# A fused spectral filter and gated FFN on one core: reordered first loads, plain-product turns, a constant filler tile, and five drains at the end

## The chip, the cores and the metric

The kernel runs on one core of one Trainium2 chip. The metric is device time in microseconds (us), lower is better. One profiled execution per kernel is quoted; its times count from the start of its span, which is about 1.8 us shorter than the device time.

Words used below: in this kernel TensorE runs the matrix products, ScalarE, VectorE and GpSimd the work on single elements, and SyncE only issues transfers and waits for semaphores. A transfer *lands* when its semaphore reports it complete. A *filler* is a matmul whose result nobody uses. The *rise* is the moment at which TensorE's granted clock goes from half to full. A *drain* is an instruction that computes nothing. The *closing checks* are SyncE's waits for semaphores at the end of the program, and its *report* is the drain with which it signals the final barrier.

## The reference

```python
x  = A_x                                   # (1, 2048, 640) bf16
xn = layernorm(x)                          # over the last axis
s  = irfft2(rfft2(xn) * (w_r + 1j*w_i))    # 2-D transform of 2048 x 640
g  = silu((gelu(xn @ w_gate) * (xn @ w_up)) @ w_down)   # F = 1536
return x + s * g
```

The sequence is split into 16 slabs of 128 rows. Gate and up projections need the input turned (rows into columns), 128 columns at a time, five pieces for a slab of 640.

## The kernel before

The kernel records every operation as a task with an estimated cost, and a planner written in Python decides the order on each engine before the program is built. So an edit of a cost, of an expected landing, or of which engine does what, can reorder work far from the edit. Parts that matter here:

```python
# fillers: matmuls on a zeroed tile that only keep TensorE busy
def blank(e):
    nc.vector.memset(place(idle, (512,)), 0.0)
...
x_in[0] = add(...)                      # slab 0 comes on ScalarE's queue
load_w(Wg, gv, g_in, 0, 2, land=4690)   # SyncE's queue, in this order
load_x(1, 2, land=5200)
load_w(Wu, uv, u_in, 0, 2, land=6790)
load_x(2, 3, land=7280)
load_x(3, 4, land=7750)
t = add(blank, "DVE", (330, 400), (0, -9), new=[idle])
t = warmed = keep_warm(6, [t])          # and 2 more after slab 0's turn
...
# turn of a raw slab: five transposes into PSUM, one copy to SBUF
for c in range(5):
    nc.tensor.transpose(out=half()[:, c*P:c*P+P], in_=X[:, n1, c*P:c*P+P], identity=ident)
...
with tc.manual_schedule():
    for t in plan.run():
        t.emit(t.on)
```

The first two tiles of gate and up work on the raw slabs and are normalised afterwards, so that TensorE need not wait for the statistics.

## Time and profile before

| quantity, kernel before | value |
|---|---|
| device time, median of the first 3 runs | 202.7 us (202.13 to 202.86) |
| span of the profiled run | 200.7 us |
| TensorE: first matmul starts, last one ends | 1.21 us, 196.76 us |
| first useful matmul, first gate matmul, first up matmul | 3.74, 5.75, 7.16 us |
| TensorE clock goes from half to full speed | 6.31 us |
| SyncE reports to the final barrier | 199.85 us |

The prediction shows the lines on which this rests.

### The profile page before, as it was taken

What the parts mean: (1) busy time and instruction counts of PE and PEld (TensorE: products, weight loads), DVE (VectorE), ACT (ScalarE), POOL (GpSimd) and SP (SyncE); (2) the same over time, 40 slices, a digit from 0 to 9 for tenths busy, and PEclk for the clock granted to TensorE, in tenths of its full rate; (3) what the DMA queues carried; (4) which work ended last, traced back from release to release, by engine and by line L of the source; (5) the groups of instructions that cost most, each with busy time, mean ns of one, the idle gap of its engine ahead of it and who ended that gap; (6) DMA issues with size and microseconds to landing.
All of it is one profiled execution on the core that took longest, in us unless ns stands there. A gap on an engine that the chain in (4) does not pass through costs nothing.

```text
span 200.7 us, 4126 instructions
## 1 busy us (share of the span) xinstructions
PE 195.5 (97%) x1527; PEld 118.2 (59%) x1527; DVE 148.6 (74%) x318; ACT 128.3 (64%) x226; POOL 32.8 (16%) x71
## 2 busy tenths in 40 slices
PE   7999999999999999999999999999999999999992
PEld 3994444667544655777755455467765555457781
DVE  3689999996524159999998999933157788787773
ACT  3899989763722767767775767233466565776451
POOL 2414333896000000000000000000004122211210
PEclk9999999999999999999999999999999999999999
DMA  6999999896639976333244110116704242332432
GB/s 180 325 316 325 339 393 225 207 257 171 207 76 349 340 179 135 92 97 122 61 118 132 68 65 1 69 64 215 309 3 141 90 134 98 102 104 92 131 103 67
DMA packets 35895, 32.63 MB, mean 163 GB/s; under 512 B 10910, under 2 KB 32930, under 8 KB 35874
## 3 DMA queue, kind: packets, MB, share of 16 engines
q1 hardware_dynamic: 34434, 29.49, 50.4%
q0 software_dynamic: 1152, 2.66, 4.9%
q10 hardware_dynamic: 288, 0.20, 0.5%
q8 instruction: 12, 0.20, 0.4%
q14 instruction: 9, 0.07, 0.1%
HBM read 22.51 MB, written 9.19 MB: 158 GB/s over the span
## 4 chain that ended last, share of the span: by engine, by line
PE 97%; DVE 0%; ACT 0%; issue 0%; DVEq 0%
PE pg L886 26%; PE pu L886 26%; PE pg L976 13%; PE pu L976 13%; PE sp L697 3%; PE sp L830 3%; PE sp L772 2%; PE sp L806 2%; PE sp L368 2%; PE sp L670 2%; PE sp L532 2%; PE sp L690 1%; PE sp L824 1%; PE sp L463 1%; PE sp L478 1%; PE sp L653 0%
## 5 line engine op out<-in xcount | busy, mean ns | idle before, releaser
L886 PE MATMUL pu<-xnT,Wu 128*128 128x512 bf16 (+1 forms) x245 | 57.6, 366 | 0.0
L886 PE MATMUL pg<-xnT,Wg 128*128 128x512 bf16 (+1 forms) x245 | 57.5, 366 | 0.0
L907 DVE TENSOR_TENSOR uT<-pu,ge 128x512 bf16<-128x512 f32 x46 | 31.8, 690 | 20.6 <-PE pu L886 17.5
L976 PEld LDWEIGHTS <-uT 128*128 128x128 bf16 x396 | 37.9, 98 | 13.5
L903 ACT ACTIVATE ge<-pg 128x512 bf16<-128x512 f32 x46 | 27.6, 599 | 24.9 <-PE pg L886 24.4
L886 PEld LDWEIGHTS <-Wg 128*128 128x128 bf16 x285 | 25.5, 99 | 22.1
L886 PEld LDWEIGHTS <-Wu 128*128 128x128 bf16 x285 | 25.0, 98 | 21.6
L976 PE MATMUL pg<-Wd,uT 128*128 128x320 bf16 (+2 forms) x204 | 30.8, 293 | 0.0
L296 ACT CAST ma<-sp 128x644 bf16<-128x644 f32 (+1 forms) x32 | 23.4, 792 | 9.7 <-PE sp L830 7.9
L976 PE MATMUL pu<-Wd,uT 128*128 128x320 bf16 (+1 forms) x192 | 29.3, 297 | 0.0
L932 POOL COPY xr<-s 1x1 bf16<-1x1 bf16 x1 | 0.2, 179 | 100.3 <-DVE s L856 100.3
L933 POOL DMA_DIRECT2D xr<-in_A_x_dram x16 | 8.8, 550 | 32.3 <-DVE res L960 30.2
L296 ACT CAST IU<-sp 128x640 bf16<-128x640 f32 x16 | 10.9, 691 | 4.2 <-PE sp L772 4.1
L296 ACT CAST Vt<-sp 128x640 bf16<-128x640 f32 x16 | 10.8, 691 | 3.7 <-PE sp L806 3.7
L296 ACT CAST mc<-sp 128x640 bf16<-128x640 f32 x16 | 10.8, 700 | 3.4 <-DMA D<-mc 2.8
L985 ACT ACTIVATE th<-pu 128x320 f32<-128x320 f32 x15 | 6.6, 438 | 9.6 <-PE pu L976 9.3
L990 DVE SCALAR_TENSOR_TENSOR G<-th,pg 128x320 bf16<-128x320 f32 x15 | 7.2, 483 | 7.1 <-ACT th L985 6.9
L985 ACT ACTIVATE th<-pg 128x320 f32<-128x320 f32 x15 | 6.7, 445 | 7.8 <-PE pg L976 7.7
L990 DVE SCALAR_TENSOR_TENSOR G<-th,pu 128x320 bf16<-128x320 f32 x15 | 7.3, 484 | 4.6 <-ACT th L985 4.4
L433 POOL TENSOR_TENSOR RSTD<-MVA,mh 128x1 f32<-128x1 f32 x12 | 9.8, 815 | 4.0 <-DVE MVA L415 3.2
L848 DVE TENSOR_TENSOR mb<-ma 128x640 bf16<-128x640 bf16 x8 | 3.9, 491 | 6.8 <-ACT ma L296 6.8
L960 DVE TENSOR_TENSOR res<-yg,xr 128x640 bf16<-128x640 bf16 (+2 forms) x18 | 8.0, 449 | 0.2
(107 smaller groups left out, 255.1 us busy)
## 6 DMA issues: line engine op xcount, KB each, us to landing
BU<-D SPq DMA_DIRECT2D x8, 640.0 KB
D<-mc SPq DMA_DIRECT2D x8, 320.0 KB
D<-IU SPq DMA_DIRECT2D x8, 320.0 KB
xr<-in_A_x_dram POOLq DMA_DIRECT2D x16, 160.0 KB, 2.6
out_dram<-res SPq DMA_DIRECT2D x15, 160.0 KB
Wg<-in_B_w_gate_dram SPq DMA_DIRECT2D x6, 320.0 KB
Wu<-in_B_w_up_dram SPq DMA_DIRECT2D x6, 320.0 KB
Wd<-in_B_w_down_dram SPq DMA_DIRECT2D x6, 320.0 KB
```

What stands on the lines that cost most here:

```text
L296: return nc.scalar.copy(out=out, in_=in_) if e == "ACT" else nc.vector.tensor_copy(out=out, in_=in_)
L433: nc.gpsimd.tensor_tensor(out=rstd, in0=var, in1=mh, op=ALU.pow)
L697: nc.tensor.matmul(into(q, ri), lhsT=sZ.tile[:, q, ri, :], rhs=FM[:, kinds[q][2] + (4 if ri and kind == 0 else 0), :], start=False, stop=T ...
L830: nc.tensor.matmul(into(q, s), lhsT=svs[s].tile[:, c, :], rhs=IM[:, q, :], start=False, stop=True, skip_group_check=True)
L886: nc.tensor.matmul(ps.tile[:, lo:hi + more], lhsT=w[:, c, t * P:(t + 1) * P], rhs=XR[:, c, lo + (lo > 0):hi + 1 if lo or more else hi] if ...
L903: nc.scalar.activation(out=ge.tile, in_=pg.tile if src is None else src, func=ACT.Gelu_apprx_tanh)
L907: nc.vector.tensor_tensor(out=u.tile, in0=pu.tile if src is None else src, in1=ge.tile, op=ALU.mult)
L933: nc.gpsimd.dma_start(out=sx.tile, in_=xv[:, n1, :])
L960: (nc.gpsimd if n1 in () else nc.vector).tensor_tensor(out=res.tile[:, lo:hi], in0=yg.tile[:, lo:hi], in1=sx.tile[:, lo:hi], op=ALU.add)
L976: nc.tensor.matmul(ps.tile[:, 0:hi - lo], lhsT=uT[grp, ks[i]].tile[:, j * P:(j + 1) * P], rhs=Wd[:, ks[i], lo:hi], start=(i == 0), stop=(i ...
L985: nc.scalar.activation(out=th.tile[:, 0:hi - lo], in_=ps.tile[:, 0:hi - lo], func=ACT.Tanh, scale=0.5)
L990: nc.vector.scalar_tensor_tensor(out=G2.tile[:, lo:hi], in0=th.tile[:, 0:hi - lo], scalar=1.0, in1=ps.tile[:, 0:hi - lo], op0=ALU.add, op1 ...
```

## The change

The intent is to give TensorE slab 1 sooner, to begin the fillers without a wait, and to shorten the end. The diff, cut:

```diff
-    def blank(e):
-        nc.vector.memset(place(idle, (512,)), 0.0)
+    ones = nc.const_aps.tensor(1.0, [P, 512], BF16)
...
-    load_w(Wg, gv, g_in, 0, 2, land=4690)
-    load_x(1, 2, land=5200)
-    load_w(Wu, uv, u_in, 0, 2, land=6790)
-    load_x(2, 3, land=7280)
-    load_x(3, 4, land=7750)
-    t = add(blank, "DVE", (330, 400), (0, -9), new=[idle])
-    t = warmed = keep_warm(6, [t])
+    load_x(1, 2, land=3990)
+    load_w(Wg, gv, g_in, 0, 2, land=4900)
+    load_x(2, 3, land=5950)
+    load_w(Wu, uv, u_in, 0, 2, land=6950)
+    load_x(3, 4, land=7450)
+    t = warmed = keep_warm(8, [], ns=395)
...
+        parts = ((0, 3), (3, 5)) if n1 < 1 else ((0, 5),)     # slab 0 in two pieces
...
+                    if n1 < 2:
+                        nc.tensor.matmul(plain(k, lo, hi)[...], lhsT=X[:, n1, c*P:c*P+P], rhs=ident, ...)
+                    else:
+                        nc.tensor.transpose(out=half(k)[...], in_=X[:, n1, c*P:c*P+P], identity=ident)
...
-    lead = ("DVE", "ACT", "DVE", "ACT")
+    lead = ('DVE', 'DVE', 'ACT', 'DVE')                       # who does the statistics
...
         for t in plan.run():
             t.emit(t.on)
+        for _ in range(5):
+            nc.sync.drain(fusable=False)
```

More of the change, by code (lines that the diff above doesn't have):

```diff
@@ L357 @@
         nc.gpsimd.memset(w[:, :, :, L:LP], 0.0)
-    idle, heat = Slot("uT"), Slot("sp")
-    def blank(e):
-        nc.vector.memset(place(idle, (512,)), 0.0)
+    heat = Slot("sp")
+    ones = nc.const_aps.tensor(1.0, [P, 512], BF16)
     def keep_warm(n, after, rank=(0, -9), ns=425):
@@ L367, in go @@
             for k in range(n):
-                nc.tensor.matmul(heat.tile[:, k % 2, :], lhsT=idle.tile[:, 0:P], rhs=idle.tile,
+                nc.tensor.matmul(heat.tile[:, k % 2, :], lhsT=ones[:, 0:P], rhs=ones,
                                  start=True, stop=True, skip_group_check=True)
-        return add(go, "PE", (n * ns, n * ns), rank, after=after, new=[] if heat.users else [heat], use=[idle] + ([heat] if heat.users else []))
+        return add(go, "PE", (n * ns, n * ns), rank, after=after, new=[] if heat.users else [heat], use=[heat] if heat.users else [])
     seq[0] += 1
-    x_in[0] = add(lambda e: None, "SP", (1, 1), (0, -5), size=1, land=3620)
-    load_w(Wg, gv, g_in, 0, 2, land=4690)
-    load_x(1, 2, land=5200)
-    load_w(Wu, uv, u_in, 0, 2, land=6790)
-    load_x(2, 3, land=7280)
-    load_x(3, 4, land=7750)
-    t = add(blank, "DVE", (330, 400), (0, -9), new=[idle])
-    t = warmed = keep_warm(6, [t])
+    x_in[0] = add(lambda e: None, "SP", (1, 1), (0, -5), size=1, land=3880)
+    load_x(1, 2, land=3990)
[4 more added lines that the diff above has]
+    t = warmed = keep_warm(8, [], ns=395)
     load_gu(2, 4)
@@ L455, in turn_raw, with half, plain, mm @@
         pt = Slot("sp")
-        def half():
-            return pt.tile[:, 0, :].bitcast(BF16)[:, 0:D]
-        def mm(e):
-            place(pt, (2, 512))
-            for c in range(5):
-                nc.tensor.transpose(out=half()[:, c * P:c * P + P], in_=X[:, n1, c * P:c * P + P], identity=ident)
-        a = add(mm, "PE", c_pe(*[140] * 5), (0, n1), after=[x_in[n1], warmed], new=[pt], use=[sX])
-        if n1 == 0:
-            keep_warm(2, [a], (0, 0, 0))
-        raw[n1] = add(lambda e: copy_on(e, XR[:, :, n1 * P + (n1 > 0):(n1 + 1) * P + (n1 > 0)], half().rearrange("p (c n) -> p c n", c=5)),
-                      {"ACT": c_act(640)} if n1 < 2 else {"ACT": c_act(640), "DVE": (415, 560)}, None, (0, n1), after=[a], use=[pt], hold={1: 1000}.get(n1, 200))
+        parts = ((0, 3), (3, 5)) if n1 < 1 else ((0, 5),)
+        t = []
+        def half(k):
+            return pt.tile[:, k, :].bitcast(BF16)[:, 0:D]
+        def plain(k, lo, hi):
+            return flat(pt.tile)[:, 512 * k:512 * k + (hi - lo) * P]
+        for k, (lo, hi) in enumerate(parts):
+            def mm(e, k=k, lo=lo, hi=hi):
+                if k == 0:
+                    place(pt, (2, 512))
+                for c in range(lo, hi):
+                    if n1 < 2:
+                        nc.tensor.matmul(plain(k, lo, hi)[:, (c - lo) * P:(c - lo) * P + P], lhsT=X[:, n1, c * P:c * P + P], rhs=ident, start=True, stop=True, skip_group_check=True)
+                    else:
+                        nc.tensor.transpose(out=half(k)[:, c * P:c * P + P], in_=X[:, n1, c * P:c * P + P], identity=ident)
+            def cp(e, k=k, lo=lo, hi=hi):
+                copy_on(e, XR[:, lo:hi, n1 * P + (n1 > 0):(n1 + 1) * P + (n1 > 0)], (plain(k, lo, hi) if n1 < 2 else half(k)[:, lo * P:hi * P]).rearrange("p (c n) -> p c n", c=hi - lo))
+            n = hi - lo
+            a = add(mm, "PE", c_pe(*[(250 if n1 < 2 else 140)] * n), (0, n1), after=[x_in[n1], warmed] + t[-1:], new=[] if k else [pt], use=[sX, pt] if k else [sX])
+            t.append(a)
+            raw[n1] = add(cp, {"ACT": c_act(128 * n)} if n1 < 2 else {"ACT": c_act(128 * n), "DVE": (83 * n, 83 * n + 145)}, None, (0, n1), after=[a], use=[pt],
+                          hold=1000 if n1 < 2 else 200)
     for n1 in range(4):
```

## The prediction

> **What bounds the kernel now.** I read the page first: the span, the busy shares, the chain that ended last.
>
> ```profile
> span 200.7 us, 4126 instructions
> ...
> PE 195.5 (97%) x1527; PEld 118.2 (59%) x1527; DVE 148.6 (74%) x318; ACT 128.3 (64%) x226; POOL 32.8 (16%) x71
> ...
> PE 97%; DVE 0%; ACT 0%; issue 0%; DVEq 0%
> ```
>
> TensorE is busy for 195.5 of 200.7 us and is 97% of the chain. It starts at 1.21 us and its last matmul ends at 196.76: 195.55 us, so it never stands still in between. I also took the start-to-start distances of all matmuls from the trace's records: from 20 to 70 us they exceed columns/2.4 + 2.5 ns by nothing, and later only concurrent small ones differ. The kernel is therefore three pieces laid end to end: a front before TensorE does useful work at full speed, about 190 us of fixed matmul work, and a tail after the last matmul. Only front, tail, or a new stall in the middle can move the time.
>
> The front, from the timeline of TensorE over the first 14 us (start, length, instruction, count), and what ScalarE does there:
>
> ```profile
> 1.21 2.74 PE L368 MATMUL sp<-uT 128*128 128x512 bf16 x6 [1.21 <-DVE uT L361]
> 3.74 0.74 PE L463 MATMUL sp<-ident,X 128*128 128x128 bf16 x5
> 4.28 1.06 PE L368 MATMUL sp<-uT 128*128 128x512 bf16 x2
> 5.27 0.69 PE L463 MATMUL sp<-ident,X 128*128 128x128 bf16 x5
> 5.75 1.00 PE L886 MATMUL pg<-XR,Wg 128*128 128x129 bf16 x10
> 6.59 0.44 PE L478 MATMUL sp<-ident,s 128*128 128x128 bf16 x5
> 6.87 0.45 PE L886 MATMUL pg<-XR,Wg 128*128 128x128 bf16 x5
> 7.16 0.73 PE L886 MATMUL pu<-XR,Wu 128*128 128x129 bf16 x10
> ```
>
> ```profile
> 4.52 0.69 ACT L296 COPY XR<-sp 128x640 bf16<-128x640 bf16 x1 [1.85 <-PE sp L463]
> 6.00 0.70 ACT L296 COPY XR<-sp 128x640 bf16<-128x640 bf16 x1 [0.78 <-PE sp L463]
> ```
>
> L368 are eight filler matmuls that only keep TensorE busy. Useful work is slab 0's five transposes (3.74), slab 1's (5.27), then ten gate matmuls (5.75). The clock is read from distances between starts: the fillers stand 0.42 us apart (2.53 / 6), half speed for 512 columns; ten gate matmuls take 0.84 us, about half of them at 107 ns and the rest at 57; from 6.59 on five take 0.28, which is 56 each. In the records the clock rises at 6.31 us. (The page's clock row shows 9 throughout and does not help here.)
>
> The waits view over 0 to 15 us names what holds the front:
>
> ```profile
> PEld L463 <- DMA X<-in_A_x_dram: 1.3, 2, 0.7
> PE sp L368 <- DVE uT L361: 1.2, 1, 1.2
> ```
>
> Slab 1 is the second of those waits. The landing records give x0 3.55 us, first gate weights 4.59, x1 5.11, first up weights 6.18, x2 6.65, x3 7.14. So x1, queued behind 320 KB of weights, comes late although the weights themselves are early. The up weights were there a microsecond before TensorE reached them.
>
> The tail, from the chain and the timeline over the last 5 us:
>
> ```profile
> 196.07 0.69 PE pg L976 x12
> ...
> 196.78 0.29 ACT G L996
> ...
> 197.09 0.29 DVE yg L953
> 197.38 0.20 DVE res L960
> ```
>
> ```profile
> 197.61 0.33 SPq L303 DMA_DIRECT2D out_dram<-res  x1
> 197.75 0.35 ACTq L965 DMA_DIRECT2D out_dram<-res  x1
> ```
>
> ```profile
> SPq L1042 <- DMA out_dram<-res: 0.8, 1, 0.8
> ```
>
> SyncE issues the last-but-one store at 197.61, then runs nine closing semaphore checks about 62 ns apart. It reaches the check of that store about 198.4 and waits 0.8 us, until 199.21. The last store's check passes at 199.37, a drain at 199.45. The next drain, which reports SyncE to the final barrier, is recorded only at 199.85, although nothing in the program stands between the two: a hole of 0.39 us where neighbours are 0.05 apart. The other engines are already waiting. 0.6 us after it begins again the DMA records show an 8 KiB transfer on the instruction queue. SyncE's earlier such transfer follows its record 80, and this hole follows record 206, about 128 instructions (8 KiB at 64 bytes) later. I read the hole as the crossing of an instruction page.
>
> **What the Trainium skill says.** "TensorE: Matmul & The Clock Gate", Part 1: start-to-start is 426.7 ns for 512 columns while cold, 215.7 once warm, and the clock rises after a busy window of about 3.4 us that runs freely, so the moment varies from run to run. The trace agrees on the distances (427 ns, 107 to 56 for 128 columns), and the rise came 5.1 us after the first matmul. The same page, Part 4: transpose-mode matmuls do not count as busy in the same way; this would be why slabs 0 and 1 become plain products. No run shows it yet, and in this trace the 3.4 us before the rise held ten transposes. "Runtime: NRT & Kernel Launch", section "Instruction fetch mechanics", has instruction memory refilled in blocks by the sequencer's own queue and the crossing "mostly hidden"; here blocks on that queue are 8 KiB and I take one crossing for unhidden. "DMA: Bandwidth & Descriptors", section on SWDGE's anatomy, puts most of the fixed cost into waiting for the last byte's receipt: here x0's last packet ended at 2.89 and it landed at 3.55.
>
> **The change part by part.**
>
> 1. Filler. The constant tile is written at 0.30, before the opening barrier. The DVE memset (0.27 us and its signal) goes. TensorE can start when the other engines do, at about 0.8 in place of 1.21. Eight fillers cold: 8 x 0.427 = 3.4, to 4.2. Their number is unchanged, but all precede slab 0; none separates the two turns.
>
> 2. Load order. x1 leads SyncE's queue and runs beside x0 on ScalarE's. It should land near x0, 3.6 to 4.0. Gate weights move from 4.59 to about 4.9; then at the steps between landings seen above (0.5 us for a slab, 1.05 for weights) x2 5.4, up weights 6.45, x3 6.95.
>
> 3. Turns and copies. A plain product streams the same 128 columns: no gain in matmul time. Slab 0 at 4.2 to 4.73, slab 1 to 5.26. Splitting slab 0 in 3 + 2 lets ScalarE copy earlier: the third product ends near 4.73, a copy of 3/5 of 640 columns is estimated at 0.46 us from the 0.69 measured, the second at 0.33. The first is done near 5.2, the second near 5.55. Gates start at 5.28 in place of 5.75, with a short wait at the fourth. F32 instead of bf16 out of PSUM: the page's own f32 copies of 640 columns are 0.69 to 0.70, so nothing.
>
> 4. What this is worth. Built, the programs have the same 3,055 TensorE rows, so matmul work is equal. In the changed order 35 useful matmuls stand ahead of the first up matmul, 30 before (slab 2's turn moved ahead). With the clock rising at 6.31 as now, gates end at 6.33, slab 2's turn 6.61, slab 1's gates 6.89, the transpose of normalised slab 0 at 7.17. TensorE reaches the up weights at 7.17 against 7.16, five matmuls ahead: 5 x 56 = 0.28 us. If the clock rises a filler earlier, gates end at 6.0 and the point comes at about 6.98: 0.28 + 0.18 = 0.46. I choose 0.4, as continuous activity begins 0.4 us sooner. The new statistics roles (slab 1 on VectorE, slab 2 on ScalarE) put four copies and slab 2's statistics on ScalarE; I expect at most a 0.1 us wait, at slab 3's turn.
>
> 5. Drains. SyncE's body grows by exactly five instructions, 196 to 201, so the page crossing moves five back: from between the last two drains to the fifth and sixth closing checks. Timing: 197.99 + five drains at about 62 ns (an estimate from the neighbouring checks) + seven checks, 0.43, + 0.39 = 199.13, still before the store's landing at 199.2. So the hole hides under the store and 0.39 - 0.05 = 0.34 us leaves the tail.
>
> Sum: 0.4 + 0.34 = 0.74, and 202.7 - 0.74 = 201.96; I say 202.0, leaving a little for new waits.
>
> **The rivals.** (a) Front only: the drains cost their own time and the hole stays, because it is not a page crossing; 202.3, or 202.6 if drains add 0.3. For: the skill calls crossings hidden. Against: the distance of 128 and the fetch. (b) The clock decides: if the activity window falls so that the rise comes late, near 7.7, all work to then costs double and front gain shrinks to about 0.2; with an early rise before's own waits at 5.27 remain and the gain grows to 0.6. The 0.73 us spread of three runs before speaks for such a lottery. (c) A new stall: the whole plan after the front was recomputed and DMA order differs for tens of us. VectorE is 74% and ScalarE 64% busy with rooms in between, so I expect none, but with TensorE full nothing can absorb one: 0.3 to 1 us back, 202.3 to 203. (d) Later gate weights bind: no, 4.9 is ahead of the copy's 5.2.
>
> **Range and chances.** Best case 0.6 + 0.34 off and a lucky median gives 201.4; front 0.2 alone gives 202.5. A 2% change is 4 us, over the whole front gap: within 2% is nearly certain.
>
> **What would show it.** First filler at 0.8 and slab 1's turn directly behind slab 0's; x1 landing before 4.1; first gate matmul near 5.3; the first up matmul near 7.0 with 35 useful ones ahead; no drain hole at the end but one among the closing checks, hidden, and about 2.75 in place of 3.09 us from the last matmul's chain end (196.76) to the report of SyncE (199.85). The prediction is wrong if TensorE stands still in the middle, or the hole stays.

## The result, and the profile after

The changed kernel takes 201.9 us (median of 4 runs, 201.79 to 201.97), before 202.57 us (4 runs, 202.13 to 202.86). The ratio is 0.9968, with a 95% interval of 0.9948 to 0.9988. Ratios are the mean time of one kernel's runs over that of the other's in the same rounds, so they are not quite the ratio of the medians. 0.65 us is clear of noise.

The page of the changed kernel:

```profile
span 200.0 us, 4106 instructions
...
PE 194.5 (97%) x1508; PEld 118.0 (59%) x1527; DVE 147.7 (74%) x319; ACT 127.5 (64%) x225; POOL 31.8 (16%) x71
...
PE 97%; issue 1%; ACT 0%; DVE 0%; DVEq 0%
```

The bound has not moved. Nineteen matmul records are missing from this trace (1508 against 1527 weight loads); each shows as a false gap of one matmul.

TensorE over the first 7 us (start, length, instruction, count):

```profile
0.77 3.57 PE L367 MATMUL sp<-const-bfloat16-1.0 128*128 128x512 bf16 x8 [0.77 <-PEq L1043]
4.16 1.13 PE L468 MATMUL sp<-ident,X 128*128 128x128 bf16 x10
5.45 0.83 PE L896 MATMUL pg<-XR,Wg 128*128 128x129 bf16 x10 [0.15 <-ACT XR L296]
6.12 0.44 PE L470 MATMUL sp<-ident,X 128*128 128x128 bf16 x5
6.39 0.45 PE L896 MATMUL pg<-XR,Wg 128*128 128x128 bf16 x5
6.72 0.45 PE L488 MATMUL sp<-ident,s 128*128 128x128 bf16 x5
```

The fillers start at 0.77 and the two turns follow each other at 4.16. Gates start at 5.45 after a wait for ScalarE's copy. The first up matmul is at 7.17, with 35 useful matmuls ahead of it (10 + 10 + 5 + 5 + 5). Two of the lines that are new in the waits view over 0 to 15 us:

```profile
PEld L896 <- DMA Wu<-in_B_w_up_dram: 0.2, 1, 0.2
PE pg L896 <- ACT XR L296: 0.2, 1, 0.2
```

The first says that the up weights now hold TensorE up. They landed at 7.12, the other landings being slab 0 4.12, slab 1 3.89, gate weights 5.10, slab 2 5.50. The clock rose at 5.03.

The end of the chain of waits in the changed kernel, and SyncE's own waits from 190 us on (total, times, longest):

```profile
195.82 0.68 PE pg L986 x12
...
196.53 0.29 ACT G L1006
...
196.84 0.29 DVE yg L963
197.13 0.20 DVE res L970
```

```profile
SPq L303 <- DVE res L970: 10.7, 5, 5.1
SPq L1054 <- PEq L1054: 0.7, 2, 0.5
```

The line that before waited 0.8 us for the store is gone: SyncE arrives at that check just as the store has landed (landing 198.94, check 198.995, one step of 64 ns behind the check ahead of it). In the records of SyncE's sequencer the hole stands between the fifth closing check (198.44) and the sixth (198.85), 0.38 us; the last two drains are 0.06 apart. From the start of the last matmul to SyncE's report it takes 2.98 us, 3.32 before.

The tail gains a little more than that. The reporting drain itself took 0.114 us in the kernel before, where it comes right behind the hole, and takes 0.007 now. From the start of the last matmul to the end of the span it is 3.74 us, 4.20 before.

So the profiled pair, whose spans differ by 0.71 us, splits into 0.25 us of front (the last matmul starts at 196.28 against 196.53) and 0.46 us of tail.

### The profile page after: what moved, and what is told of

It reads as the page before. It is cut to its first block, busy times and chain, and to the rows that moved or that the text cites. A ratio compares the mean times of both kernels' runs of the same rounds, so it can differ in the third digit from the quotient of the medians.

```text
span 200.0 us, 4106 instructions
## 1 busy us (share of the span) xinstructions
PE 194.5 (97%) x1508; PEld 118.0 (59%) x1527; DVE 147.7 (74%) x319; ACT 127.5 (64%) x225; POOL 31.8 (16%) x71
## 4 chain that ended last, share of the span: by engine, by line
PE 97%; issue 1%; ACT 0%; DVE 0%; DVEq 0%
PE pu L896 26%; PE pg L896 25%; PE pg L986 13%; PE pu L986 13%; PE sp L707 3%; PE sp L840 3%; PE sp L782 2%; PE sp L816 2%; PE sp L680 2%; PE sp L367 2%; PE sp L542 2%; PE sp L834 1%; PE sp L700 1%; PE sp L488 1%; PE sp L543 0%
## 5 line engine op out<-in xcount | busy, mean ns | idle before, releaser
L896 PE MATMUL pg<-xnT,Wg 128*128 128x512 bf16 (+1 forms) x231 | 55.7, 365 | 0.5
L986 PE MATMUL pu<-Wd,uT 128*128 128x320 bf16 (+1 forms) x192 | 29.8, 297 | 0.0
L296 ACT CAST Z<-sp 128x1024 bf16<-128x1024 f32 x8 | 7.9, 1013 | 2.5 <-PE sp L680 2.5
L431 POOL TENSOR_TENSOR RSTD<-MVA,mh 128x1 f32<-128x1 f32 x12 | 8.2, 686 | 2.8 <-DVE MVA L413 2.1
L409 DVE BATCH_NORM_STATS2 STAT<-X 128x6 f32<-128x320 bf16 x12 | 5.5, 482 | 3.7 <-DMA X<-in_A_x_dram 3.7
```

Of the source, the lines that this page charges most:

```text
L296: return nc.scalar.copy(out=out, in_=in_) if e == "ACT" else nc.vector.tensor_copy(out=out, in_=in_)
L409: nc.vector.bn_stats(out=STAT[:, n1, 6 * g:6 * g + 6], in_=x[:, 320 * g:320 * g + 320])
L431: nc.gpsimd.tensor_tensor(out=rstd, in0=var, in1=mh, op=ALU.pow)
L896: nc.tensor.matmul(ps.tile[:, lo:hi + more], lhsT=w[:, c, t * P:(t + 1) * P], rhs=XR[:, c, lo + (lo > 0):hi + 1 if lo or more else hi] if ...
L986: nc.tensor.matmul(ps.tile[:, 0:hi - lo], lhsT=uT[grp, ks[i]].tile[:, j * P:(j + 1) * P], rhs=Wd[:, ks[i], lo:hi], start=(i == 0), stop=(i ...
```

## The experiments

Twelve kernels ran in three calls, each beside fresh runs of the kernel before on the same chip. All were correct. Six runs each, eleven of before per call (medians 202.69, 202.73, 202.59).

To compare fronts I use one number: the moment by which TensorE has reached 35 useful matmuls. It is the start of the first up matmul, plus 56 ns for each useful matmul short of 35 ahead of it.

| kernel | ratio to before (95%) | clock rise | first gate | 35 useful by | last matmul starts | to SyncE's report |
|---|---|---|---|---|---|---|
| before | 1 | 6.31 | 5.75 | 7.43 | 196.53 | 3.32 |
| changed | 0.9968 (0.9948 to 0.9988) | 5.03 | 5.45 | 7.17 | 196.28 | 2.98 |
| before + 5 drains at the end | 0.9973 (0.9953 to 0.9993) | 4.67 | 5.61 | 7.13 | 196.22 | 2.97 |
| before + 5 drains in the middle | 0.9983 (0.9967 to 1.0) | 6.67 | 6.12 | 7.80 | 196.89 | 2.98 |
| changed, no drains | 0.9991 (0.9975 to 1.0007) | 5.26 | 5.44 | 7.13 | 196.36 | 3.31 |
| changed, transposes again | 0.9972 (0.9952 to 0.9993) | 3.39 | 5.11 | 6.94 | 196.26 | 2.97 |
| changed, old load order | 1.0033 (1.0009 to 1.0057) | 5.39 | 5.79 | 7.28 | 197.95 | 2.98 |
| changed, memset tile, 7 fillers | 0.9982 (0.9966 to 0.9997) | 4.71 | 5.59 | 7.11 | 196.29 | 2.98 |
| changed, up weights ahead of slab 2 | 1.0011 (0.9989 to 1.0033) | 5.14 | 5.44 | 7.15 | 197.16 | 2.97 |
| changed, slab 0 in one piece | 0.9979 (0.9965 to 0.9994) | 5.54 | 5.73 | 7.30 | 196.41 | 2.98 |
| changed again | 0.9966 (0.995 to 0.9983) | 3.38 | 4.93 | 7.05 | 196.57 | 2.97 |
| before + early fillers + 5 drains | 0.9973 (0.996 to 0.9986) | 3.97 | 5.49 | 7.00 | 196.36 | 2.98 |
| changed, plain small fillers | 1.0016 (0.9994 to 1.0039) | 4.72 | 5.34 | 7.31 | 198.18 | 2.98 |
| changed, transposed small fillers | 1.0031 (1.0007 to 1.0054) | 5.11 | 5.34 | 6.85 | 198.11 | 2.99 |

The rise is one sample per kernel, from the records of the granted clock. All times in the last five columns are of the one profiled run.

The middle can be read from the same table, as the time from 35 useful matmuls to the start of the last matmul. It is 189.09 to 189.11 us in the kernel before, in its two variants with the plan unchanged and drains added, in the changed kernel and in the one with slab 0 in one piece; 189.2 to 189.5 in five others, the changed kernel's second profile (189.52) among them; and 190.0 to 191.3 in four, of which more below.

### The tail: three runs that move or remove the drains

The theory was that the hole is the crossing of an instruction page; the rival, that it belongs to the last drain, or that draining at the end is what helps.

```diff
 # kernel before, drains at the end
         for t in plan.run():
             t.emit(t.on)
+        for _ in range(5):
+            nc.sync.drain(fusable=False)
```

> The kernel before with only the five SyncE drains added after its last store; nothing else moves. Theory (the 0.39 us hole between SyncE's last two drains is an instruction-page crossing, and five more instructions move it under the wait for the last stores): the hole is found between the fifth and sixth closing checks, the last two drains stand about 0.06 us apart, the stretch from TensorE's chain end to SyncE's report shrinks from 3.09 to about 2.75 us, and the time falls by about 0.34 us (ratio 0.9983). Rival (the hole is a fixed cost of the last drain, hidden or not): hole unchanged, time the same or up to 0.3 us longer (ratio 1.0000 to 1.0015).

The median was 201.92 us, ratio 0.9973. The stretch from the last matmul to the report went from 3.32 to 2.97, the hole (0.385 us) stands ahead of the sixth check. The time fell by 0.77 us by the medians, more than the 0.34 expected (the interval holds both). Of the 0.76 us between the profiled spans 0.46 are tail; the other 0.30 are front, which this edit did not touch, in a run whose clock rose at 4.67.

```diff
 # changed kernel
-        for _ in range(5):
-            nc.sync.drain(fusable=False)
```

> The changed kernel without its five drains. Theory (page crossing): the hole of about 0.39 us is back between the last two drains, and of the 0.65 us gain only the front's 0.26 to 0.3 is left (ratio to before about 0.9987). Rival (the drains do nothing, all of the gain is the front): ratio stays at about 0.997 and there is no hole.

The median was 202.32 us, ratio 0.9991. The hole is back between the last two drains (0.386 us), the stretch is 3.31, and SyncE's waits from 190 us on show the store again:

```profile
SPq L303 <- DVE res L970: 10.6, 5, 5.1
SPq L1052 <- DMA out_dram<-res: 0.8, 1, 0.8
SPq L1052 <- PEq L1052: 0.7, 2, 0.5
```

```diff
 # kernel before, drains some 30 SyncE instructions ahead of the end
-        for t in plan.run():
+        for k, t in enumerate(plan.run()):
             t.emit(t.on)
+            if k == 700:
+                for _ in range(5):
+                    nc.sync.drain(fusable=False)
```

> The kernel before with five SyncE drains in the middle of its queue (some 30 SyncE instructions before its end, in a stretch where SyncE is idle for over 10 us), none at the end. Theory (only the count of instructions ahead of the end matters, since it sets where the page boundary falls): same effect as at the end, the hole moves to between the fifth and sixth closing checks and the time falls by about 0.34 us. Rival (what helps is the draining at the end itself, for instance by the last store being flushed earlier): hole stays at the end at 0.39 us, time as before (ratio 1.000).

The median was 202.27 us, ratio 0.9983. Nothing was drained at the end, and the hole still moved ahead of the sixth check (0.381 us) and the stretch is 2.98. Its SyncE waits from 190 us on:

```profile
SPq L1045 <- PEq L1045: 0.7, 2, 0.5
SPq L1045 <- DMA out_dram<-res: 0.4, 1, 0.4
```

The wait for the store is down from 0.8 to 0.4: the hole has eaten the other half. This settles the tail: what counts is the number of SyncE instructions ahead of the end, not what they do. Every kernel with five more has a stretch of 2.97 to 2.99, both kernels without have 3.31 to 3.32; to the end of the span these are 3.73 to 3.75 and 4.19 to 4.20. The effect is 0.34 us up to the report and 0.45 us in all. In every one of the fourteen profiles the hole stands behind SyncE's 207th record, whatever comes there. In the two kernels whose plan gives SyncE one record less (old load order, up weights ahead of slab 2) it stands one check later. That the boundary is one of instruction pages rests on this fixed count and on the 8 KiB transfer that follows; no record names it.

### The front: plain products or transposes

```diff
-                    if n1 < 2:      # plain product
+                    if n1 < 0:      # all slabs by transposes; copies follow suit
```

> The changed kernel with slabs 0 and 1 turned by transpose-mode matmuls again, same order, same copies, everything else as changed. Theory A (transposes do not count as activity and so put off the clock's rise): the rise comes later than the 5.03 us of the changed kernel, by up to a window of 3.4 us, and the time grows by 0.1 to 0.4 us. Theory B (transposes count, or the window's phase alone decides): rise between 4 and 7 us as the window falls, time within 0.1 us of the changed kernel, ratio to before about 0.997.

The median was 201.95 us, ratio 0.9972, within 0.1 us of the changed kernel. But the rise fell at 3.39, ahead of the turns, so this profile cannot tell whether transposes delay it. I therefore replaced the fillers themselves.

```diff
-                nc.tensor.matmul(heat.tile[:, k % 2, :], lhsT=ones[:, 0:P], rhs=ones, ...)
+                for c in range(3):      # control: 24 products of 128 columns
+                    nc.tensor.matmul(heat.tile[...], lhsT=ones[:, 0:P], rhs=ident, ...)
```

> Control for the next: the changed kernel with its fillers made of 24 plain products of 128 columns against the identity (which is ready near 1.5 us, so they fill 1.5 to 4.1). Nothing else differs. Expected under both theories: the clock rises between 3.4 and 6.0 us, as in the other profiles of this front (3.4 to 5.5), and the time is within 0.2 us of the changed kernel.

```diff
+                    nc.tensor.transpose(out=..., in_=ones[:, 0:P], identity=ident)   # in its place
```

> The same 24 fillers in transpose mode, all else equal to the control. Theory A (transpose-mode matmuls do not count as activity for the clock): counted activity begins only with slab 0's plain products at 4.1, so the rise comes 2.5 us later than in the control, at 5.9 or after in every run, and the time grows by 0.3 to 1 us. Theory B (they count): rise between 3.4 and 6.0 and time as the control within 0.2 us.

TensorE of the run with transposed fillers:

```profile
1.52 2.72 PE L368 MATMUL sp<-ident,const-bfloat16-1.0 128*128 128x128 bf16 x24 [1.52 <-POOL ident L351]
4.03 1.24 PE L468 MATMUL sp<-ident,X 128*128 128x128 bf16 x10
5.34 0.83 PE L896 MATMUL pg<-XR,Wg 128*128 128x129 bf16 x10
```

The rise came at 5.11, against 4.72 in the control. Theory A asked for 5.9 or later and falls. The argument is stronger than one lucky sample: in the 3.41 us up to the rise only 1.07 us was plain products (4.03 to 5.10), 31% of the window; in the kernel before, the window that ended at 2.90 held 1.7 us of plain products (from 1.21), half of it, and no rise followed, nor did one follow 2.04 us of them (1.21 to 3.25) in the run with drains in the middle. So the transposes must have counted. (That the window is 3.41 us long fits the traces: the full clock lasted 194.56 or 197.97 us in every profile, 57 and 58 times 3.413. That the fillers ran in transpose mode is taken from the call; the trace prints both kinds alike.) So nothing here shows that the plain products of the change bought an earlier clock.

The expected times were both missed: 203.02 and 203.40 us, 0.9 and 1.3 us longer than the changed kernel on the same chip, whose program order they share. The reason lies in the middle. Waits of TensorE between 8 and 190 us in the run with transposed fillers:

```profile
PE sp L542 <- DVE mb L529: 1.4, 1, 1.4
PE sp L542 <- ACT mc L296: 0.3, 1, 0.3
```

In the changed kernel's profile that view is empty. Followed back between 28 and 52 us, again with transposed fillers:

```profile
DVE s L445 <- POOL RSTD L431: 2.5, 1, 2.5
POOL D L614 <- DMA D<-in_A_w_r_dram: 2.3, 1, 2.3
```

In GpSimd's records the reciprocal deviation of a late slab (RSTD, at 48.60) comes behind DMA issues that wait for earlier weight rows to land. In the changed kernel's profile that wait is 0.6 us, and VectorE waits 0.8 for RSTD without harm to TensorE; here it is 2.3, and TensorE stands still for 1.4 us, from 50.95 to 52.40. The control has the same pattern (0.9 and 0.5 us). What lengthened that wait in these two I did not find.

### The front: load order, split copy, start of the fillers

```diff
 # changed kernel, loads in the order of before, with before's landings (cut)
-    load_x(1, 2, land=3990)
-    load_w(Wg, gv, g_in, 0, 2, land=4900)
-    load_x(2, 3, land=5950)
-    load_w(Wu, uv, u_in, 0, 2, land=6950)
+    load_w(Wg, gv, g_in, 0, 2, land=4690)
+    load_x(1, 2, land=5200)
+    load_w(Wu, uv, u_in, 0, 2, land=6790)
+    load_x(2, 3, land=7280)
...
```

> The changed kernel with the load order of before (gate weights, slab 1, up weights, slab 2, slab 3) and the plan that follows from it: 25 useful matmuls ahead of the first up matmul. Theory A (the new load order is what the front gains from): slab 1 lands near 5.1 again, gates start near 5.7, and the time rises by about 0.3 us, to the level of the kernel before with drains in its slow clock phase (span 200.3 to 200.7). Theory B (the load order only exchanges one wait for another: the up weights land at about 6.2 in place of 7.1): time as the changed kernel, within 0.1 us (span 200.0 to 200.2).

The median was 203.34 us, ratio 1.0033: worse than both theories. Slab 1 landed at 5.45, gates started at 5.79, but the up weights were there at 6.54 and 35 useful matmuls were reached at 7.28, only 0.11 later than the changed kernel. Most of the rest is again the middle (1.6 us longer by the table), since the planner made another order:

```profile
PE sp L542 <- DVE mb L529: 0.7, 1, 0.7
...
PE sp L542 <- ACT mc L296: 0.5, 1, 0.5
```

So this run prices the load order at 0.1 us in the front and cannot price it in the total.

```diff
 # changed kernel, up weights loaded ahead of slab 2
-    load_x(2, 3, land=5950)
-    load_w(Wu, uv, u_in, 0, 2, land=6950)
-    load_x(3, 4, land=7450)
+    load_w(Wu, uv, u_in, 0, 2, land=6700)
+    load_x(2, 3, land=7100)
+    load_x(3, 4, land=7600)
```

> A try at a better one: the changed kernel with the up weights loaded ahead of slab 2, and the plan that follows (25 useful matmuls ahead of the first up matmul). Theory A (the late up weights, 7.1 us, are what the front still waits for): they land near 6.5, the first up matmul is near 6.6 to 6.7, with 25 done, which is up to 0.1 us better than 35 at 7.17 (35 - 25 = 10 x 56 ns = 0.56). Theory B (one wait replaces another: slab 2 then comes late): same time, or 0.1 us longer.

The median was 202.72 us, ratio 1.0011, no improvement. The up weights landed at 6.50 and the first up matmul started at 6.59 with 25 ahead: 7.15, equal to the changed kernel's 7.17. Removing that wait gained nothing in the front, and the new plan's middle is 0.9 us longer, 0.5 of it in the same wait for a VectorE sum (L542 on mb).

```diff
-        parts = ((0, 3), (3, 5)) if n1 < 1 else ((0, 5),)
+        parts = ((0, 5),)
```

> The changed kernel with slab 0 turned and copied in one piece, not 3 + 2. Theory A (the slack ahead of the up weights hides it): gates start near 5.75 in place of 5.45, the first up matmul stays near 7.15, time within 0.1 us of the changed kernel. Theory B (the copy is on the path): 0.3 us longer.

The median was 202.12 us, ratio 0.9979. Gates started at 5.73, as theory A expected, but the first up matmul at 7.30, 0.14 later than in the changed kernel, with a rise 0.5 us later; the ratios differ by about 0.2 us, within their intervals. This lies between the two theories, and the plan changed too, so what the split is worth stays open.

```diff
-    ones = nc.const_aps.tensor(1.0, [P, 512], BF16)
+    ones = IM.rearrange("p a b -> p (a b)")[:, 0:512]
+    nc.vector.memset(ones, 1.0)
...
-    t = warmed = keep_warm(8, [], ns=395)
+    t = warmed = keep_warm(7, [], ns=450)
```

> The changed kernel with a filler tile written by a VectorE memset, so that TensorE starts at 1.21 in place of 0.77, and seven fillers in place of eight, so that slab 0's turn begins at the same 4.2. Theory A (an earlier start of activity brings an earlier clock rise): the rise, or how often the run falls into the late phase, is worse; on average 0.1 to 0.3 us longer. Theory B (the moment of the rise is set by the free-running window, and slack before the up weights absorbs cold matmuls): within 0.1 us of the changed kernel.

The first filler started at 1.48 (1.21 was expected). The median was 202.39 us, ratio 0.9982, some 0.3 to 0.5 us longer than the changed kernel, which is theory A's side; but its profiled run is one of its fast ones (201.8 us, rise 4.71, 35 useful by 7.11) and looks like the changed kernel's. So the times speak for A, and no trace shows why. A late rise is not the reason, at least in the longest run (201.0 us of span): its mean granted clock of 0.996 puts the rise near 4.9 us (how, is told under the fronts below). This one is inconclusive.

```diff
 # kernel before, two parts of the change alone
+    ones = nc.const_aps.tensor(1.0, [P, 512], BF16)
...
-            for k in range(n):          # 6 fillers ahead of slab 0
+            for k in range(7 if n == 6 else n):
...                                      # on `ones` in place of the zeroed tile
+        for _ in range(5):
+            nc.sync.drain(fusable=False)
```

> The kernel before with two parts of the change alone: fillers on the constant tile (so TensorE starts at 0.77, seven fillers ahead of slab 0 so that its turn begins no later than 3.9) and the five drains; load order, turns and roles as before. Theory A (an earlier start of activity, so an earlier rise, is the front's share): as good as the changed kernel, ratio near 0.9965, rise before 6.0, first up matmul near 6.85 with 30 useful ahead. Theory B (the load order and the split are the front's share): 0.2 to 0.3 us longer than the changed kernel, ratio near 0.998.

```diff
 # changed kernel, unaltered
```

> The changed kernel unaltered, for its time and clock rise on the same chip as the other three. Theory A (the front's gain is an earlier clock rise on average, since activity starts 0.44 us earlier and nothing interrupts it): rise at or before 6.0, ratio to before near 0.9965, of which 0.0017 is the drains. Theory B (the front gained nothing but luck): ratio near 0.9983, the drains alone.

On the same chip the changed kernel had 202.09 us (201.41 to 202.25), ratio 0.9966, and before with early fillers and drains 202.12 us (201.73 to 202.34), ratio 0.9973. The intervals overlap almost entirely. With before's load order, its transposes and its undivided copy, that kernel reached 35 useful matmuls at 7.00, ahead of the changed kernel's 7.05 and 7.17. No run beat the changed kernel clearly.

### What the fronts say together

The first up matmul of two kernels with before's load order and an early rise, the kernel before with five drains at the end and the one with early fillers, both with 30 useful matmuls ahead:

```profile
6.85 0.56 PE L886 MATMUL pu<-XR,Wu 128*128 128x129 bf16 x7
```

```profile
6.72 0.73 PE L887 MATMUL pu<-XR,Wu 128*128 128x129 bf16 x10
```

The two profiles with before's front and a late rise (6.31, 6.67) reached 35 useful matmuls at 7.43 and 7.80; in the second, slab 0's turn also began 0.4 us later (4.14). The same load order with an early rise (4.67, 3.97) reached them at 7.13 and 7.00. Fronts of the changed kind, rises from 3.38 to 5.54, did at 6.85 to 7.31. At an early rise the two fronts are thus alike within the spread, and before's loses about 0.3 us (7.43 against 7.13) when the rise is late. These few profiles suggest that the moment of the rise, not the load order, is the larger part of what a pair of them shows as the front's gain.

What sets the moment stays open. The eight profiles whose fillers start at 0.77 all have a rise by 5.54, and of the three that start at 1.21 two are later than 6, which would suit the earlier start as the cause. But the three that start near 1.5 rose at 4.71, 4.72 and 5.11, which does not, and each profile is one draw. All fourteen fit one reading, made after the fact and tested by no run: the rise ends the first 3.41 us window in which TensorE was busy long enough, and where the windows fall is chance. The window that ended with the rise at 3.38 held 2.62 us of matmuls (from 0.76), which sufficed; 2.04 us in the run with drains in the middle did not. No changed front was seen with a late rise, so what it would then cost is open as well.

The runs without a trace say a little more, by their mean granted clock. As the fourteen profiles show, it is below 1.000 when the clock has fallen to half again before the span ends. As the full clock lasted 194.56 us or more, a mean of 0.998 or less puts the rise before about 6 us; 1.000 can be either. Of the eleven runs of the kernel before in the first call, the four with 0.998 or less have the shortest spans, 200.3 to 200.6 us against 200.9 to 201.2, as if the rise decided. But in the third call seven such runs spread over 200.4 to 201.2 (in the second there are two, 200.7 and 200.9, among 200.5 to 201.2). So an early rise alone does not make a run short.

In the times, the front's share is the 0.9991 of the changed kernel without drains, about 0.2 us, with an interval that includes none. The kernel before with nothing but the drains has 0.9973, against 0.9968 for the whole change: no time on record separates the two.

## Why the prediction was right, point by point

- **The total.** 202.0 predicted, 201.9 measured, a fall of 0.67 us by the medians against 0.7 predicted. The mechanism of the tail was right, that of the front was not borne out. That the sum came so close is partly luck: 0.40 + 0.34 was predicted for front and tail, the profiled pair shows 0.25 + 0.46.
- **Drains.** Predicted a hole moved to between the fifth and sixth checks and 0.34 us gained; measured exactly there, 0.34 to 0.35 us up to the report, and three runs confirm the cause. The prediction stopped at the report: the reporting drain behind the hole also shrank from 0.114 to 0.007 us, which makes the tail's gain 0.46. The estimate of 62 ns a drain was off in shape: the first took 0.185 us to the next, the others about 0.052, 0.40 in all for five. The margin of 0.08 us ahead of the store's landing was used up; with a few instructions more SyncE would come late.
- **Fillers and turns.** First filler predicted 0.8, measured 0.77; turns back to back at 4.2, measured 4.16. Right.
- **First gate.** Predicted 5.28, measured 5.45: the step that failed is "Splitting slab 0 in 3 + 2 lets ScalarE copy earlier". The third product ended at 4.66, yet the first copy started only at 4.91, just after the fifth ended at 4.88, and ran to 5.40. In the built program that copy waits for a TensorE count which is raised only behind all five products, and the second copy has no wait of its own. So the split lets the gates begin after a shorter copy, but not the copy begin earlier. Slab 1 landed at 3.89, inside the 3.6 to 4.0 given, but slab 0, beside it on the other queue, at 4.12 where it had landed at 3.55 before; the prediction gave no new time for it. The fillers ended at about the same moment, so this hardly held up its turn here.
- **The up weights.** This is the mis-sized term. Predicted to land at 6.45; measured 7.12 here, 6.79 to 7.26 in the other runs with this load order. The gap from slab 2 to the up weights was 1.6 us in the changed kernel, not 1.05; in four other runs the gap was 1.0 to 1.2, but slab 2 itself came at 5.7 to 6.2, not 5.4. For a clock that rises one filler earlier I had given 6.98 and a front gain of 0.46 (the "gates end at 6.0" in that sum is a slip: by its own steps it is 6.14). The clock rose earlier still, at 5.03, but TensorE waited for the weights until 7.17 and the front gained 0.25 in this pair. But the run with the up weights moved forward shows that undoing this wait alone gains nothing. Why they land so late is open.
- **The mechanism of the front.** I gave the gain to the load order and the work it puts ahead of the up weights. The runs don't bear that out: before's own front equals the changed one when the clock rises early. The five more matmuls that stand ahead of the up weights were real, but these weights landed at 7.12, 0.7 to 0.9 us later than in the kernel before and its variant with drains (6.18, 6.43), which took the gain back. Rival (b), the clock lottery, was named as a rival and fits what the profiles of the front show, but not its size: for an early rise it gave a gain of 0.6 us, and the profiles show none (7.17 against 7.13). The reading of the skill's line on transposes, offered as the reason for plain products, fell.
- **A new stall.** Rival (c) did not occur in the changed kernel's first profile. In its second the waits view shows 0.2 us, and the middle was 0.4 us longer. In four of the altered kernels waits of 0.5 to 1.7 us appeared, and the middle was 0.9 to 2.2 us longer. The remark that with a full TensorE nothing absorbs a wait was right.

## What to carry to other kernels

When one engine is full from first matmul to last, price a change as front plus tail, and look at the sequencer's own records at the tail: a hole of 0.4 us between two trivial instructions may be moved under a wait by changing how many instructions come ahead of it. Measure such a gain to the end of the span, not to the last instruction that you had in mind. Before crediting a reordered load, compare profiles in which the clock rose at about the same moment, because here fronts with the old load order differed by more among themselves than from the new one. And where a planner orders the work, an edit at the start can open a wait 50 us later, so read the whole waits view of the full engine, not only the part that was edited.

## What the Trainium skill lacked or had wrong

- "TensorE: Matmul & The Clock Gate", Part 4, says that transpose-mode matmuls do not count as busy in the same way for the clock. Here the clock rose at 5.11 us with 24 transposes from 1.52 to 4.03 and only 1.07 us of plain products in the 3.41 us ahead of the rise, where 1.7 and 2.04 us of plain products alone had not sufficed in the kernel before and its variant with drains in the middle. The measurement decides, though it is one profile: they counted.
- "Runtime: NRT & Kernel Launch", section "Instruction fetch mechanics", calls the crossing of a block mostly hidden and gives blocks of 16 KiB (256 instructions). If the hole is such a crossing, it was an exposed 0.38 to 0.39 us at the very end of the kernel before. It stood some 126 SyncE records after the place at which an earlier transfer of the instruction queue shows, and the transfers on that queue are 8 KiB (those of 16 KiB go over another).
- I found no page with the distance between drains that a program itself adds to SyncE's queue: the first of five took 0.185 us to the next, the others about 0.052 us.
- I found no page with a price for arithmetic that stands behind a waiting DMA issue on GpSimd: a 2.3 us wait for a landing came ahead of a reciprocal deviation, and TensorE then stood still for 1.4 us.
